# A sparse-attention and SwiGLU kernel: one identity copy moved from VectorE to ScalarE, and eight weight loads of 256 columns made into four of 512

## The chip, the cores and the metric

The kernel runs on one core of a Trainium2 chip. A core has a matrix engine (TensorE, PE in the profile), VectorE (DVE), ScalarE (ACT), GpSimd (POOL), and SyncE (SP), which here only issues DMAs. Each engine works through its own queue of instructions in order. Sixteen DMA engines move the data. The metric is the device time of one execution in microseconds.

## What is computed

Two stages follow each other. The first is block-sorted attention: for each of 4 batches and 8 heads an 8 x 8 matrix is normalised five times over rows and columns (Sinkhorn), its rows mix the eight 96-row blocks of k and v, and each block of q attends to its mixed block of k. The second is a SwiGLU feed-forward layer on the 3072 rows of 512 that come out.

```
P = sort_net
for _ in range(5):
    P = exp(P - max(P, -1));  P = P / sum(P, -1);  P = P / sum(P, -2)
k_sorted = einsum('bhij,bhjcd->bhicd', P, k_blocks)      # v the same
attn = softmax(q_blocks @ k_sorted.T / sqrt(64));  x = attn @ v_sorted
g = x @ w_gate;  val = x @ w_val                          # 512 -> 1536
out = (g * sigmoid(g) * val) @ w_out                      # 1536 -> 512
```

## The kernel before

All inputs lie in memory as 32-bit floats and are converted to bfloat16 by the DMAs that load them, which GpSimd issues (`load_v`, `load_k`, `load_q`, `load_gv`, and one load for `wo_sb`). The order of TensorE's and GpSimd's queues is the order of the program text, over the whole kernel; for VectorE and ScalarE that holds up to line 515, and later a scheduler orders them.

The start goes as follows. GpSimd issues the two halves of v of batch 0 (lines 134 and 135), builds the 128 x 128 identity `ident` (136), issues q and the four pieces of k of batch 0 (137 to 139), and then copies parts of v into `vch`, which holds v with its last two axes exchanged (140 to 142). A copy of one element of k's last piece into `landed` (144) makes it wait there until k is in. Then come the weight loads: `load_gv(lo, hi)` issues two DMAs, columns lo to hi of the gate weights into `wg_sb` and the same columns of the value weights into `wv_sb` (lines 145 to 149, with `load_v(1)` after column 1024). Behind them in the queue stand k and q of batch 1 and `wo_sb` (150 to 152), then the copies of v of batch 1 (573). The DMAs go around over eight completion semaphores, so an issue also waits for the load that used its semaphore eight loads earlier.

Meanwhile VectorE and ScalarE run the Sinkhorn loop (lines 183 to 200) on the tile `p_ps`: an exponential by ScalarE (184), then row sum, reciprocal, product, column sum, reciprocal, product by VectorE (194 to 200). In the second iteration VectorE also builds `mask` from `ident` (187) and copies a 64 x 64 corner of `ident` into the mixing matrix `rmix[0]` (188). That matrix is what TensorE multiplies k and q of batch 0 with (line 233): its upper half mixes k by P, its lower half passes q through. In the third and fourth iteration, and twice after the loop, ScalarE also takes its share of the copies into `vch` (`copy_v` with `nc.scalar`, lines 190, 192, 206 and 207). TensorE fills this time with matmuls on zeros (416, 420), some of them tied to the row sums (425).

Then v and k of batch 0 are mixed (`v_chunk`, `kq_chunk`), the scores, exponentials and products with v follow (`qk`, `av`), and the first half batch enters the feed-forward layer. The layer runs in eight passes n of 384 rows. A pass goes over twelve blocks m of 128 hidden columns: `gate(n, m)` (line 355 the matmuls, 363 tanh by ScalarE, 365 the product by VectorE) and `value(n, m)` (373 and 378). The blocks of pass 0 take their weights in column order: block m needs columns 128 m to 128 m + 127 of both matrices. Blocks 0 and 1 are started by `early` (497); the rest of pass 0 comes from `ffn(0)`, merged with attention work of the same batch by `merge`, which places side work by a running sum of costs. The product with `wo_sb` (390) of pass n comes in pass n + 1.

Of the kernel before, what the change touches and what calls it, by code (L numbers as in the profile page):

```python
# [17 lines left out]
def kernel(  # L18
# [11 lines left out]
    nc = tc.nc  # L30
# [9 lines left out]
    DF = moe_w_gate.shape[1]  # L40
# [50 lines left out]
    def load_k(b, lo, hi):  # L91
        rows = highr if b else lowr
        nc.gpsimd.dma_start(out=kq_tile(b)[rows, lo:hi, :], in_=k_nat[b, :, lo:hi, :])
# [10 lines left out]
    def load_v(b, lo, hi):  # L104
        if b // 2 not in v_tiles:
            v_tiles[b // 2] = vnp.tile([128, C, D], BF16, name=f"v{b // 2}", tag="vn")
        u = b % 2
        nc.gpsimd.dma_start(out=v_tiles[b // 2][u * R:(u + 1) * R, lo:hi], in_=v_nat[b, :, lo:hi, :])

    def load_w(sb, dram, lo, hi):  # L110
        nc.gpsimd.dma_start(out=sb[:, :, lo:hi], in_=dram[:, :, lo:hi])

    def load_gv(lo, hi):
        load_w(wg_sb, wg_dram, lo, hi)
        load_w(wv_sb, wv_dram, lo, hi)

    def copy_v(eng, pair, rows, s, n=4, d0=0, d1=D):
        cs = slice(s * (C // n), (s + 1) * (C // n))
        dst = vch3[rows, d0:d1, cs]
        src = v_tiles[pair][rows, cs, d0:d1]  # L120
        if eng is nc.scalar:
            eng.copy(dst, src.transpose([0, 2, 1]))
        else:
            eng.tensor_copy(dst, src.transpose([0, 2, 1]))  # L124

    ident = const.tile([128, 128], BF16)
    lowr, highr = slice(0, R), slice(R, 2 * R)
# [14 lines left out]
    copy_v(nc.gpsimd, 0, lowr, 5, 8, 40, D)  # L142
    landed = const.tile([R, 1], BF16)
    nc.gpsimd.tensor_copy(landed, kq_tiles[0][0:R, C - 1, D - 1:D])
    for m in range(0, 1024, 256):
        load_gv(m, m + 256)
    load_v(1, 0, C)
    for m in range(1024, DF, 256):
        load_gv(m, m + 256)
    load_k(1, 0, C)  # L150
    load_q(1, 0, C)
    nc.gpsimd.dma_start(out=wo_sb, in_=wo_dram)
# [1 line left out]
    rmix = {b: const.tile([128, 2, H, NB], BF16, name=f"rmix{b}") for b in (0, 1, "p")}  # L154
# [28 lines left out]
    for it in range(N_ITER):  # L183
        nc.scalar.activation(p_ps, p_sb if it == 0 else p_ps, AF.Exp)
        if it == 1:
            with nc.allow_low_precision("0/1 mask"):
                nc.vector.tensor_reduce(mask, id4, axis=AX.XY, op=ALU.add)
            nc.vector.tensor_copy(rmix[0][highr, 1].rearrange("p h i -> p (h i)"), ident[highr, highr])
        if it == 2:
            copy_v(nc.scalar, 0, lowr, 2, 8)  # L190
        if it == 3:
            copy_v(nc.scalar, 0, lowr, 3, 8)
        rowred = rowreds[it]
        nc.vector.reduce_sum(rowred[:, :, 0], p_ps, axis=AX.X)
        nc.vector.reciprocal(rowred, rowred)
        nc.vector.tensor_mul(p_ps, p_ps, rowred.to_broadcast([BH, NB, NB]))
        nc.vector.reduce_sum(colred[:, 0, :], p_ps.transpose([0, 2, 1]), axis=AX.X)
        nc.vector.reciprocal(colred, colred)
        if it < N_ITER - 1:
            nc.vector.tensor_mul(p_ps, p_ps, colred.to_broadcast([BH, NB, NB]))  # L200
# [428 lines left out]
```

## Time and profile before

Three runs gave 249.53, 249.59 and 250.57 us, a median of 249.59. The profiled execution has a span of 248.0 us; its own time beyond the span isn't recorded with the page, and the median lies 1.6 us above the span.

| what | us |
|---|---|
| median of the runs | 249.59 |
| span of the profiled execution | 248.0 |
| DVE busy | 157.7 |
| ACT busy | 110.3 |
| POOL busy | 52.5 |
| gate matmuls L355 | 76.5 |
| value matmuls L373 | 77.3 |
| output matmuls L390 | 64.0 |

Busy time is the time in which an engine executes; issuing a DMA doesn't count. The chain that ended last is followed back from the last instruction: at each step it goes to what released the instruction, or to the one before it on the same engine. In a timeline, the columns are the start in us, the length in us, the engine, the line of the kernel, the operation, the tile written and the tiles read, shapes and types, and how many instructions were merged; in brackets stands idle time of the engine before it and what ended it. A row for a DMA issue gives the issuing engine, the number of issues, the size and the time from the issue to the landing.

### The profile page before, as it was taken

How to read it: one execution, taken by the hardware profiler on the slowest of the kernel's cores; microseconds unless marked ns; L12 is line 12 of the kernel's file. 1: busy time of each engine (PE TensorE's matmuls, PEld its weight loads, DVE VectorE, ACT ScalarE, POOL GpSimd, SP SyncE). 2: the span in 40 equal slices, each digit the busy share in tenths (PEclk: the TensorE clock that was granted, in tenths of full speed). 3: DMA queues.
4: the chain of work that ended last, by engine and by line, in shares of the span. 5: the costliest groups of instructions: out<-in, count | busy, mean ns of one | idle time of the engine just before them, and what ended most of it. 6: DMA issues, size and time to landing. Idle time of an engine off the chain costs nothing.

```text
span 248.0 us, 6193 instructions
## 1 busy us (share of the span) xinstructions
PE 240.1 (97%) x2636; PEld 141.3 (57%) x2636; DVE 157.7 (64%) x332; ACT 110.3 (44%) x187; POOL 52.5 (21%) x47
## 2 busy tenths in 40 slices
PE   7899999999999999999999999999999999999994
PEld 6376566666555556655555655565555555555543
DVE  6778689887555775857657646755764585446700
ACT  2977553453544444454642552354244334232311
POOL 7948459960059200000000000000000000000000
PEclk9999999999999999999999999999999999999999
DMA  5959999999999296010122121112111121100122
GB/s 101 211 95 166 215 189 228 194 226 211 221 170 192 53 210 164 3 42 3 45 54 52 57 62 34 44 42 78 32 42 45 39 57 55 42 22 24 42 81 88
DMA packets 39530, 24.38 MB, mean 98 GB/s; under 512 B 27728, under 2 KB 35664, under 8 KB 38992
## 3 DMA queue, kind: packets, MB, share of 16 engines
q0 software_dynamic: 21328, 14.16, 38.9%
q1 hardware_dynamic: 18176, 9.84, 14.1%
q8 instruction: 20, 0.33, 0.5%
q14 instruction: 6, 0.05, 0.1%
HBM read 28.32 MB, written 7.86 MB: 146 GB/s over the span
## 4 chain that ended last, share of the span: by engine, by line
PE 83%; DVE 7%; ACT 3%; issue 3%; DMA 2%; DVEq 0%; ACTq 0%; POOLq 0%
PE v_ps L373 23%; PE o_ps L390 23%; PE g_ps L355 22%; PE tkq L233 4%; PE av_ps L304 3%; PE qk L277 2%; DVE gs_sb L365 2%; DMA v<-in_v_dram 2%; DVE st L310 2%; PE tv L245 2%; PE idle_ps L416 1%; DVE h L378 1%; PE o_ps L406 1%; ACT th_sb L363 1%; PE x_ps L321 1%
## 5 line engine op out<-in xcount | busy, mean ns | idle before, releaser
L365 DVE SCALAR_TENSOR_TENSOR gs_sb<-th_sb,g_ps 128x384 bf16<-128x384 bf16 x96 | 52.8, 550 | 51.8 <-ACT th_sb L363 49.1
L373 PE MATMUL v_ps<-xt,wv_sb 128*128 128x384 bf16 x380 | 77.3, 326 | 0.7 <-DVE gs_sb L365 0.4
L355 PE MATMUL g_ps<-xt,wg_sb 128*128 128x384 bf16 x376 | 76.5, 326 | 0.0
L363 ACT ACTIVATE th_sb<-g_ps 128x384 bf16<-128x384 f32 x96 | 47.1, 490 | 56.0 <-PE g_ps L355 53.5
L390 PE MATMUL o_ps<-wo_sb,h 128*128 128x512 bf16 x276 | 64.0, 379 | 0.0
L378 DVE SCALAR_TENSOR_TENSOR h<-v_ps,gs_sb 128x384 bf16<-128x384 f32 x96 | 53.3, 556 | 6.6
L373 PEld LDWEIGHTS <-wv_sb 128*128 128x128 bf16 x380 | 35.4, 97 | 24.6 <-issue 2.3
L355 PEld LDWEIGHTS <-wg_sb 128*128 128x128 bf16 x376 | 34.6, 97 | 23.2 <-issue 0.3
L390 PEld LDWEIGHTS <-h 128*128 128x128 bf16 x276 | 26.3, 98 | 28.9
L395 ACT COPY o_sb<-o_ps 128x512 f32<-128x512 f32 x23 | 13.5, 585 | 50.8 <-PE o_ps L390 50.8
L124 POOL COPY vch<-v 64x1536 bf16<-64x1536 bf16 (+2 forms) x11 | 28.6, 2639 | 20.7 <-DMA v<-in_v_dram 20.7
L290 ACT ACTIVATE e_all<-qk 96x768 bf16<-96x768 f32 x30 | 22.6, 802 | 8.1 <-PE qk L277 8.1
L310 DVE TENSOR_TENSOR st<-av_ps,r_sb 96x512 bf16<-96x512 f32 x32 | 21.7, 679 | 0.2
L304 PEld LDWEIGHTS <-e_all 96*128 96x128 bf16 x256 | 12.2, 98 | 4.9 <-ACT e_all L290 0.8
L304 PE MATMUL av_ps<-vt,e_all 96*128 96x65 bf16 x256 | 13.5, 194 | 0.0
L211 DVE CAST vt<-tv 96x1024 bf16<-96x1024 f32 (+1 forms) x9 | 9.8, 1100 | 2.7 <-PE tv L255 1.6
L308 DVE RECIPROCAL r_sb<-av_ps 96x8 f32<-96x8 f32 x32 | 6.4, 199 | 7.6 <-PE av_ps L304 7.5
L213 ACT CAST vt<-tv 96x1024 bf16<-96x1024 f32 (+1 forms) x9 | 9.2, 1032 | 3.1 <-PE tv L255 1.8
L211 DVE CAST kqt<-tkq 128x1024 bf16<-128x1024 f32 (+1 forms) x7 | 7.5, 1068 | 2.7 <-PE tkq L233 2.6
L213 ACT CAST kqt<-tkq 128x1024 bf16<-128x1024 f32 (+1 forms) x7 | 6.0, 894 | 6.6 <-PE tkq L233 6.6
L416 PE MATMUL idle_ps<-warm_sb 128*128 128x512 bf16 x28 | 8.7, 409 | 0.0
L233 PE MATMUL tkq<-rmix,kq 128*64 128x64 bf16 x384 | 7.8, 197 | 0.6 <-issue 0.6
(74 smaller groups left out, 126.3 us busy)
## 6 DMA issues: line engine op xcount, KB each, us to landing
out_dram<-o_sb SPq DMA_DIRECT2D x23, 256.0 KB, 2.0
v<-in_v_dram POOLq DMA_DIRECT2D x3, 768.0 KB, 19.9
kq<-in_q_dram POOLq DMA_DIRECT2D x2, 768.0 KB, 13.6
wg_sb<-in_moe_w_gate_dram POOLq DMA_DIRECT2D x6, 256.0 KB, 8.5
wv_sb<-in_moe_w_val_dram POOLq DMA_DIRECT2D x6, 256.0 KB, 9.1
wo_sb<-in_moe_w_out_dram POOLq DMA_DIRECT2D x1, 1536.0 KB, 23.8
kp<-in_k_dram POOLq DMA_DIRECT2D x2, 768.0 KB, 15.1
q_scr<-in_q_dram POOLq DMA_DIRECT2D x2, 768.0 KB, 29.9
```

Of the source, the lines that this page charges most:

```text
L124: eng.tensor_copy(dst, src.transpose([0, 2, 1]))
L211: nc.vector.tensor_copy(dst, src)
L233: nc.tensor.matmul(tp[two * D:(two + 1) * D, lc, :], lhsT=kq_tiles[b][:, at + lc, :], rhs=rm[:, two], start=True, stop=True)
L290: nc.scalar.activation(e_all[:, n:n + 2, 0:4 * C], wide[0:C, :, 0:4 * C], AF.Exp, scale=scale)
L304: nc.tensor.matmul(o[:, two, i4, :], lhsT=e[:, i4 * C:i4 * C + 128], rhs=vt[:, 2 * g + two, half * 4 + i4, :], start=True, stop=True)
L310: nc.vector.tensor_tensor(st.rearrange("p i two d -> p two i d"), o[0:C, :, :, 0:D], r_sb.to_broadcast([C, 2, 4, D]), op=ALU.mult)
L355: nc.tensor.matmul(g_ps, lhsT=wg_sb[:, kc, ts(m, 128)], rhs=xt[:, kc, :], start=(kc == 0), stop=(kc == NKC - 1))
L363: nc.scalar.activation(th_sb, g_ps, AF.Tanh, scale=0.5)
L365: nc.vector.scalar_tensor_tensor(gs_sb, th_sb, 1.0, g_ps, op0=ALU.add, op1=ALU.mult)
L373: nc.tensor.matmul(v_ps, lhsT=wv_sb[:, kc, ts(m, 128)], rhs=xt[:, kc, :], start=(kc == 0), stop=(kc == NKC - 1))
L378: nc.vector.scalar_tensor_tensor(h_tiles[n][:, m, :], v_ps, 0.5, gs_tiles.pop(m), op0=ALU.mult, op1=ALU.mult)
L390: nc.tensor.matmul(o_ps, lhsT=h_w[:, m, ts(t3, 128)], rhs=wo_sb[:, m, :], start=(m == 0), stop=(m == NFC - 1))
```

## The change

The copy of the identity corner goes from VectorE's queue to ScalarE's, between the second and the third exponential. The gate and value weights of columns 0 to 511 are loaded as before, those from column 512 on in loads of 512 columns: gate 512 to 1023, value 512 to 1023, v of batch 1, gate 1024 to 1535, value 1024 to 1535. That is eight weight loads rather than twelve, for the same bytes.

```
-    for m in range(0, 1024, 256):
-        load_gv(m, m + 256)
+    load_gv(0, 256)
+    load_gv(256, 512)
+    load_gv(512, 1024)
     load_v(1, 0, C)
-    for m in range(1024, DF, 256):
-        load_gv(m, m + 256)
+    load_gv(1024, DF)
...
-            nc.vector.tensor_copy(rmix[0][highr, 1].rearrange("p h i -> p (h i)"), ident[highr, highr])
+            nc.scalar.copy(rmix[0][highr, 1].rearrange("p h i -> p (h i)"), ident[highr, highr])
```

On the other engines the order of instructions stays what it was.

## The prediction

> **What bounds the kernel now.** I read the page first, for the engine shares and the DMA queues; then the chain of waits around the stage in which the first edit sits; then the timelines of VectorE, TensorE and GpSimd over the first 45 us, with the landing times of the weight loads.
>
> ```profile
> PE 240.1 (97%) x2636; PEld 141.3 (57%) x2636; DVE 157.7 (64%) x332; ACT 110.3 (44%) x187; POOL 52.5 (21%) x47
> PE   7899999999999999999999999999999999999994
> DMA  5959999999999296010122121112111121100122
> q0 software_dynamic: 21328, 14.16, 38.9%
> ```
>
> TensorE is busy for 97% of the span, from about 25 us on without a gap that matters. Its order is written out by hand, so a stall of TensorE in there moves all that follows. The DMA engines are full from slice 2 to slice 13 (6.2 us each). Whatever is asked for in that stretch lands in queue order, and asking sooner brings nothing.
>
> The first edit sits ahead of that, in the Sinkhorn loop, where TensorE runs filler. The chain of waits there:
>
> ```profile
> 1.27 4.98 DMA v<-in_v_dram
> 6.25 0.02 issue
> 6.28 1.53 ACT vch L122
> 7.81 0.12 ACT p_ps L184
> ```
>
> Up to 7.9 us the end is set by the landing of the first half of v (1.27 + 4.98 = 6.25), then by ScalarE's transposing copy of it, then by the fourth exponential, which stands behind that copy on ScalarE. VectorE's first two iterations are not in the chain. Its timeline:
>
> ```profile
> 3.84 0.22 DVE L200 TENSOR_TENSOR p_ps<-p_ps,colred 32x64 f32<-32x64 f32 x1
> 3.98 0.26 DVE L187 TENSOR_REDUCE mask<-ident 128x8 bf16<-128x128 bf16 x1
> 4.26 0.32 DVE L188 COPY rmix<-ident 64x64 bf16<-64x64 bf16 x1
> 4.61 0.21 DVE L194 TENSOR_REDUCE rowred<-p_ps 32x8 f32<-32x64 f32 x1
> ...
> 7.47 0.22 DVE L200 TENSOR_TENSOR p_ps<-p_ps,colred 32x64 f32<-32x64 f32 x1
> ```
>
> **The copy on ScalarE: what it removes.** In the second iteration the row sum L194 starts 0.77 us after L200 (4.61 - 3.84); the timeline has 0.48 us in the third iteration (6.28 - 5.80) and in the fourth (7.95 - 7.47). So the copy costs VectorE 0.29 us here, and without it L200 of the third iteration would start at 7.18 rather than 7.47 and the fourth exponential could follow at 7.44. But line 190's copy is ahead of that exponential in ScalarE's queue. It starts at 6.28 because v lands at 6.25, and its 1.53 us end at 7.81. The exponential started at 7.73 (successive ScalarE instructions overlap by 0.07 to 0.08 in the timeline: 7.73 + 0.19 against 7.85) and can't start sooner by more than 0.02. What is late next is therefore DMA, and the 0.29 us becomes waiting. I take a gain of 0.02. Its bounds are 0 and 0.29; the whole would need v to land by 5.96.
>
> **What it adds.** ScalarE gets one 64x64 copy. The trace has none from SBUF at this size there; the nearest rows are w_sb<-w_ps 64x64 at 0.21 us (L446) and 64x128 at 0.26 us (L447). I take 0.21. It would run from 4.31 to 4.52, while ScalarE sits idle for 1.78 us before the third exponential at 6.06 (5.77 then). Queued behind it is only that exponential, and 1.25 us of cover remain; without the cover it would cost 0.21. It needs ident, which GpSimd finishes at 3.04 (2.75 + 0.29). The sum for this edit is -0.02.
>
> **The weight loads: what is removed.** Eight loads of 256 columns, 256 KB each as written, become four of 512 KB. GpSimd spends 0.74 to 0.80 us on the issue of each. If a wide one costs the same (the row of wo, with three times the rows, took 1.05), four issues or some 3 us go; the bounds are 2 us and 3 us. None of it reaches the end: after its last issue GpSimd waits 2.62 us for v of batch 1 anyway. Behind these issues in its queue stand load_v(1), load_k(1), load_q(1) and wo. They are issued sooner into a full queue, and land when their bytes come.
>
> **What is moved: the landings.** A load reports as a whole. The value weights of column 1024, needed first, came in a load of their own and now wait for those of column 1535. Issues and landings, from GpSimd's timeline and the DMA view of each issue:
>
> ```profile
> 25.85 0.74 POOL L111 DMA_DIRECT2D wg_sb<-in_moe_w_gate_dram  x1 [0.59 <-DMA wv_sb<-in_moe_w_val_dram]
> 27.25 0.74 POOL L111 DMA_DIRECT2D wv_sb<-in_moe_w_val_dram  x1 [0.66 <-DMA wg_sb<-in_moe_w_gate_dram]
> ...
> wv_sb<-in_moe_w_val_dram POOLq DMA_DIRECT2D x1, 256.0 KB, 13.7
> wo_sb<-in_moe_w_out_dram POOLq DMA_DIRECT2D x1, 1536.0 KB, 23.8
> ```
>
> The last value load landed at 27.25 + 13.7 = 40.95. In the same way the four loads of columns 512 to 1023 landed at 26.95, 28.29, 29.62 and 31.05 (gate and value in turn), v at 34.78, and the last four at 35.99, 37.22, 38.55 and 40.95. Bytes keep their order except that gate's second half now goes before value's first. At the old rate the four new loads land where the second of each pair did: gate 512 at 28.29, value 512 at 31.05, gate 1024 at 37.22, value 1024 at 40.95. TensorE first needs them at 31.61, 32.61, 38.48 and 39.13, the starts of hidden blocks 4 and 8:
>
> ```profile
> 32.61 0.81 PE L373 MATMUL v_ps<-xt,wv_sb 128*128 128x384 bf16 x4
> ...
> 38.48 0.81 PE L355 MATMUL g_ps<-xt,wg_sb 128*128 128x384 bf16 x4
> 39.13 0.81 PE L373 MATMUL v_ps<-xt,wv_sb 128*128 128x384 bf16 x4
> ```
>
> Three keep a margin (3.3, 1.6 and 1.3 us). The fourth was 1.91 us early (39.13 - 37.22) and would be 1.82 us late. Two things change this.
>
> First, rows twice as long move faster. The wo load has the new row length. By bandwidth, the stretch from 35 to 38 us (narrow loads) moved 199 GB/s and that from 48 to 53 us (wo) 209: 2 MB take 10.5 or 10.0 us, 0.5 saved. By landings, wo came 7.02 us after q (31.29 + 23.8 = 55.09, against 29.87 + 18.2 = 48.07), 2.34 us for each 512 KB; four narrow loads at the pace of 35.99 to 38.55 (1.28) make 2.56. Over four wide loads that saves 0.9; at the slower pace of 25.52 to 31.05 (1.38, or 2.76 a pair) it would be 1.7. Bounds: 0 and 1.7. TensorE waits for landings, so I take 0.9: 40.05.
>
> Second, the last value load took 2.40 us after the one before it, against 1.28: 1.1 us of irregularity. Between 36 and 39 us the instruction queue has one 16 KB packet with 1.9% of 16 engines' 3 us, so 0.9 us of one engine. I take that fetch to follow the program, which is nearly the same after, so I leave the 1.1 us in; without it the load would land at 38.95, and nothing would be late.
>
> A weight load normally lies under the matmul before it; one that waits shows its 0.10 us (the page's 97 ns). The stall is 40.05 + 0.10 - 39.13 = 1.02 us, with bounds of 0 and 1.92 (40.95 + 0.10 - 39.13). Behind it stand the whole rest of TensorE's queue, and ScalarE, VectorE and the stores that feed on it. The chain of waits runs on TensorE alone from 30.96 to 61 us, so no gap gives the stall back. Sum: 1.02 - 0.02 = 1.0 us.
>
> **Rules against the rows.** Landings of narrow loads lie 1.28 us apart because they queue behind each other without a fixed price. [...]
>
> **The sum.** The page gives the span, 248.0; the median of the runs, 249.59, is 1.6 above it, which I take as constant around the span. Span 249.0, time 250.6.
>
> **The rivals.** (a) The stall of about 0.4 to 1.25 us, as summed: 250.6, chance 0.45. (b) Hidden anyway: wide rows and no irregularity, the load in time for block 8. For it speaks that only the last landing in the row of loads was uneven; against it that margin would be 0.1 to 0.2 us. Time 249.6, chance 0.21. (c) Slower by a measurable amount: the wide load brings no rate, the DMA engines being bound by what they read, and value 1024 lands at 40.95 or later, 1.8 us after TensorE wants it. For it speaks the step of only 199 to 209 GB/s. It decides from a landing after 40.28 (39.13 + 1.25 - 0.10). Time 251.4, chance 0.27. (d) The first edit does what it says: v lands earlier than in this profile, 0.29 us comes through, and the weights are in time: 249.3, chance 0.03. (e) Faster by something no row shows, 248.0: chance 0.04.
>
> **How the numbers follow.** A measurement of this kernel can tell some 0.5%, 1.25 us, from no change: below 248.34 faster, above 250.84 slower. Faster is (e), 0.04; slower is (c) and a little of (a), 0.28; the rest, 0.68, is the same. The range runs from 249.4, below (b) and near (d), to 251.6, just past the upper bound of the stall (249.59 + 1.92 = 251.5).
>
> **What would show it.** Right: the fourth exponential still at 7.7 us, with ScalarE waiting for DMA; a single TensorE gap of about 1 us ahead of block 8's value matmuls, released by the DMA of wv_sb, which lands near 40. Wrong: no gap there, or gaps at block 4 too, or a p_ps chain 0.29 us earlier at line 203. The time would be wrong if landings shift by more than a microsecond between executions.

## The result, and the profile after

The changed kernel took 251.92 us as the median of six runs (251.22 to 253.06), the kernel before 249.84 (six runs, 249.53 to 250.57). The ratio is 1.0081, with an interval of 1.0054 to 1.0107: slower by 2.1 us, and outside the range that was given. The profiled execution took 251.52 us with a span of 249.7, so 1.8 us lie outside the span. For the kernel before that was put at 1.6, as its median less the span of its profile; but executions of it with a span of 248.0 took 250.02 to 250.09 us in the batches of the experiments, so some 2.05 lie outside, and the profile came from an execution about 0.45 us slower than the median of 249.59. One of the twelve executions of e2 below (256.29 us, at a mean granted clock of 0.978) was in a slower state than the others and isn't counted.

From the page of the changed kernel, the shares of the engines, the DMA packets and the group of the value matmuls (busy us, mean ns of one, then idle time ahead and what ended it):

```profile
PE 237.6 (95%) x2611; PEld 141.2 (57%) x2636; DVE 157.6 (63%) x331; ACT 110.5 (44%) x188; POOL 49.5 (20%) x43
DMA packets 37418, 24.38 MB, mean 98 GB/s; under 512 B 27664, under 2 KB 33552, under 8 KB 36880
L373 PE MATMUL v_ps<-xt,wv_sb 128*128 128x384 bf16 x380 | 77.3, 326 | 3.2 <-DMA wv_sb<-in_moe_w_val_dram 2.5
```

GpSimd's 3 us are gone (52.5 to 49.5, x47 to x43: for GpSimd the page does count the issues of DMAs as busy time), as worked out, and so are 2112 DMA packets (39530 to 37418). The value matmuls now have 2.5 us of idle time that a weight load ended. Where it stands is seen in the chain of waits and in TensorE's timeline:

```profile
21.97 18.97 DMA wv_sb<-in_moe_w_val_dram
40.94 0.05 issue
40.99 0.82 PE v_ps L373 x4
```

```profile
24.23 0.48 PE L497 MATMUL g_ps<-xt,wg_sb 128*128 128x384 bf16 x2
...
37.71 0.81 PE L355 MATMUL g_ps<-xt,wg_sb 128*128 128x384 bf16 x4
40.99 0.82 PE L373 MATMUL v_ps<-xt,wv_sb 128*128 128x384 bf16 x4 [2.46 <-DMA wv_sb<-in_moe_w_val_dram]
```

The gap is where it was forecast: ahead of block 8's value matmuls, and nowhere else in the feed-forward layer's first pass. Two of its terms were not what was forecast. The load landed at 40.94, no sooner than the last narrow load of before. And TensorE came to the feed-forward layer at 24.23 instead of 25.00, so it was ready for block 8's values at 38.36 (37.71 + 0.65) instead of 39.13. It lost 40.99 - 38.36 = 2.63 us there, less the 0.77 that it had come sooner: 1.86, against 1.7 in the spans.

ScalarE's timeline in the Sinkhorn loop:

```profile
4.32 0.24 ACT L188 COPY rmix<-ident 64x64 bf16<-64x64 bf16 x1
5.79 0.19 ACT L184 ACTIVATE p_ps<-p_ps 32x64 f32<-32x64 f32 x1 [1.22 <-DVE p_ps L200]
6.20 1.52 ACT L122 COPY vch<-v 64x768 bf16<-64x768 bf16 x1 [0.23 <-DMA v<-in_v_dram]
7.63 0.20 ACT L184 ACTIVATE p_ps<-p_ps 32x64 f32<-32x64 f32 x1
```

The third exponential is 0.27 us sooner (5.79 against 6.06). Then ScalarE waits 0.23 us for v, and the fourth is 0.10 sooner (7.63 against 7.73), of which 0.08 is v's own landing (6.20 against 6.28). The moved copy took 0.24 us and nothing waited for it.

### The profile page after: what moved, and what is told of

It is laid out like the page before. It is cut to its first block, busy times and chain, and to the rows that moved or that the text cites. A ratio compares the mean times of both kernels' runs of the same rounds, so it can differ in the third digit from the quotient of the medians.

```text
span 249.7 us, 6164 instructions
## 1 busy us (share of the span) xinstructions
PE 237.6 (95%) x2611; PEld 141.2 (57%) x2636; DVE 157.6 (63%) x331; ACT 110.5 (44%) x188; POOL 49.5 (20%) x43
## 2 busy tenths in 40 slices
DMA packets 37418, 24.38 MB, mean 98 GB/s; under 512 B 27664, under 2 KB 33552, under 8 KB 36880
## 4 chain that ended last, share of the span: by engine, by line
PE 73%; DMA 12%; DVE 5%; POOL 4%; issue 3%; ACT 2%; DVEq 0%; POOLq 0%
PE o_ps L390 22%; PE v_ps L373 21%; PE g_ps L355 20%; DMA wv_sb<-in_moe_w_val_dram 8%; DMA kq<-in_k_dram 4%; PE tkq L233 3%; PE av_ps L304 2%; DVE gs_sb L365 2%; PE qk L277 2%; DVE h L378 1%; POOL wg_sb L111 1%; PE o_ps L406 1%; DVE st L310 1%; DVE vt L211 1%; POOL wv_sb L111 1%
## 5 line engine op out<-in xcount | busy, mean ns | idle before, releaser
L390 PE MATMUL o_ps<-wo_sb,h 128*128 128x512 bf16 x255 | 61.5, 379 | 1.3 <-issue 0.3
L233 PEld LDWEIGHTS <-kq 128*64 128x64 bf16 x384 | 6.8, 112 | 1.8 <-issue 1.5
```

The lines of the kernel that those rows point to most:

```text
L233: nc.tensor.matmul(tp[two * D:(two + 1) * D, lc, :], lhsT=kq_tiles[b][:, at + lc, :], rhs=rm[:, two], start=True, stop=True)
L390: nc.tensor.matmul(o_ps, lhsT=h_w[:, m, ts(t3, 128)], rhs=wo_sb[:, m, :], start=(m == 0), stop=(m == NFC - 1))
```

## The experiments

All ratios are to the kernel before, run on the same chip among the others, with 95% intervals. Four chips were used, one each for e1 to e4, e5 to e8, e9 and e10, and e11 and e12; the kernel before had medians of 249.71 to 250.07 on them, so medians of different batches compare to some 0.4 us only. The landing is that of the load with the value weights of column 1024; for the kernel before and the copy alone, the last value load's landing stands in brackets.

| run | ratio | median us | gap at block 8 in the profile, us | landing, us |
|---|---|---|---|---|
| before | 1 | 249.84 | 0 | 37.22 (40.95) |
| the change | 1.0081 (1.0054 to 1.0107) | 251.92 | 2.46 | 40.94 |
| e1 copy alone | 1.0004 (0.9978 to 1.0030) | 250.03 | 0 | 38.38 (42.26) |
| e2 wide loads alone | 1.0093 (1.0055 to 1.0131) | 251.43 | 1.19 | 40.03 |
| e3 middle pair wide | 0.9994 (0.9971 to 1.0017) | 249.53 | 0 | 36.99 |
| e4 last pair wide | 1.0137 (1.0081 to 1.0193) | 253.82 | 2.24 | 40.80 |
| e5 change, filler in the gap | 1.0074 (1.0045 to 1.0104) | 251.56 | 0.86 after the filler | 41.51 |
| e6 last values narrow again | 1.0019 (0.9993 to 1.0045) | 250.37 | 0.50 | 39.33 |
| e7 middle wide, v in halves | 0.9989 (0.9968 to 1.0011) | 249.58 | 0 | 35.91 |
| e8 change, v in halves | 1.0000 (0.9975 to 1.0025) | 249.57 | 0.20 | 38.59 |
| e9 a third of wo first | 1.0054 (1.0034 to 1.0075) | 251.36 | 1.73 | 40.60 |
| e10 narrow, v in halves | 0.9995 (0.9976 to 1.0013) | 249.65 | 0 | 35.64 |
| e11 e4 with filler | 1.0083 (1.0049 to 1.0118) | 251.83 | 0.15 after the filler | 40.96 |
| e12 e4 again, beside e11 | 1.0129 (1.0076 to 1.0181) | 253.71 | 2.38 | 41.27 |

### Which edit, and which load

The first four separate the parts. e1 has only `nc.scalar.copy` in line 188, e2 only the wide loads. e3 and e4 have the copy and one wide pair each:

```
e3:  load_gv(512, 1024); load_v(1, 0, C); load_gv(1024, 1280); load_gv(1280, DF)
e4:  load_gv(512, 768); load_gv(768, 1024); load_v(1, 0, C); load_gv(1024, DF)
```

> Copy on ScalarE alone, all weight loads 256 columns wide. Theory A (the copy takes a hole out of the k mixing): the 0.57 us gap of TensorE near 17 us in the profile of before is gone, the first gate matmul (line 497) starts near 24.2 instead of 25.0, and the time falls by 0.6 to 0.8 us, ratio 0.997. Theory B (the hole is chance of the one profile): the Sinkhorn chain gives at most 0.1 us, ratio 0.9995 to 1.000, and the hole is there in some profiles and not in others.

> Wide loads alone, the copy on VectorE as before. Both theories: one TensorE gap ahead of block 8's value matmuls, released by the load of wv_sb, which lands near 40.9. Theory A: TensorE arrives at 39.1, the gap is 1.8 to 1.9 us and the time rises by that, ratio 1.0075. Theory B: arrival is between 38.4 and 39.1 by chance, and the end is set by the landing alone, so this kernel takes as long as the whole change, ratio 1.008.

> Copy on ScalarE, columns 512 to 1023 in wide loads, columns from 1024 on in loads of 256. If the last pair of wide loads alone makes the stall, there is no gap at block 8 and the time is that of the copy alone, ratio 0.997 to 1.000; the value load of 512 to 1023 lands near 31.2, ahead of block 4 (32.6 or 31.8). If the middle pair has a part in it, a gap shows at block 4, or block 8's loads land later than 36 and 37.2.

> Copy on ScalarE, columns 512 to 1023 in loads of 256, columns from 1024 on in wide loads. If the last pair makes the whole stall: a gap of 1.8 to 2.5 us ahead of block 8's value matmuls and the time of the whole change, ratio 1.007 to 1.008. If wide rows of the middle pair had saved any landing time, the last load would land up to 0.5 later here than in the whole change (40.9).

The copy alone changes nothing that can be measured. The gap near 17 us is still in its profile, at 0.34 us, so theory A falls. Wide loads alone are as slow as the whole change by the ratio; their median of 251.43 says less, because the eleven executions fall into two groups (250.60 to 251.43 and 253.27 to 254.25), which the next section takes up. The middle pair costs nothing in e3, as its margins of 3.3 and 1.6 us said, and the last pair makes the loss. TensorE's timeline in e2, e3 and e4, in this order:

```profile
40.08 0.82 PE L373 MATMUL v_ps<-xt,wv_sb 128*128 128x384 bf16 x4 [1.19 <-DMA wv_sb<-in_moe_w_val_dram]
```

```profile
38.33 0.81 PE L374 MATMUL v_ps<-xt,wv_sb 128*128 128x384 bf16 x4
```

```profile
40.84 1.20 PE L374 MATMUL v_ps<-xt,wv_sb 128*128 128x384 bf16 x4 [2.24 <-DMA wv_sb<-in_moe_w_val_dram]
```

In e3 the block starts at 38.33 and waits for nothing. In e4 two things stand out: a median 1.9 us above that of the change, and four matmuls that take 1.20 us instead of 0.82.

### The clock after the wait

Those longer matmuls led to e5 and, later, to the pair e11 and e12. The filler is one line among the side work of pass 0, ahead of `value(0, 8)`; it computes nothing that is used:

```
+            if n == 0 and m == 8:
+                todo.append((0.0, lambda: fill(bank_tile("gap_ps", "x"), 9)))
```

> The whole change, with nine filler matmuls of 128x512 (0.22 us each, 1.9 us in all) in TensorE's queue between block 8's gate and value matmuls, where the wait for the load lies. If the wait alone sets the end (1.2 to 2.5 us by the landing), the filler lies inside it and the time is 251.2 to 251.5, as in the undisturbed runs of the change. If a part of the change's time comes from the granted clock falling after the wait (half clock for 3.4 us in the profile of the wide last pair alone, worth 1.7 us), that part goes: no execution with a mean clock of 0.993, none above 252, and the median is 251.3 against 251.9 for the change and 252.3 for wide loads alone. If the clock has nothing to do with it, the spread up to 254 stays.

> The wide last pair alone (as in e4) with nine filler matmuls (2.1 us) in TensorE's queue between block 8's gate and value matmuls. If the clock falls because TensorE is idle there, few executions or none have a mean granted clock of 0.993, and the median is 251.2 to 251.6, about what the executions of e4 at full clock took (251.5 and 251.7). If the fall has another cause, about half or more stay at 0.993 and the median near e12's.

> The same kernel as e4, beside e11 on the same chip: half or more of the executions at a mean clock of 0.993 and 253 to 255 us, the others at 1.000 and 251 to 252; median 252.5 to 254.

The view by stages of e12 (busy us and count of each engine, then PEclk, the granted clock, DMA share and GB/s):

```profile
39.00:41.00 2.00, 0.00 (x0) 0.00 (x0) 0.80 (x2) 0.47 (x1) 2.00 (x2) 1.00 1.11 221
41.00:42.00 1.00, 0.68 (x4) 0.46 (x5) 0.00 (x0) 0.00 (x0) 1.00 (x2) 0.90 1.00 209
42.00:43.00 1.00, 1.00 (x12) 0.69 (x10) 0.17 (x2) 0.00 (x0) 1.00 (x1) 0.50 1.00 209
43.00:44.00 1.00, 1.00 (x5) 0.50 (x4) 1.00 (x3) 0.00 (x0) 1.00 (x1) 0.50 1.10 233
44.00:45.00 1.00, 1.00 (x5) 0.47 (x4) 0.42 (x2) 0.49 (x1) 1.00 (x2) 0.50 1.04 221
45.00:46.00 1.00, 1.00 (x10) 0.60 (x8) 0.63 (x3) 0.00 (x0) 1.00 (x1) 0.89 0.76 154
```

TensorE is idle from 39 to 41 us and works again at 41.32, after a wait of 2.38 us for the weights; from 41.80 to 45.22 the clock is at half. The lost shares, 0.10 + 0.50 + 0.50 + 0.50 + 0.11, make 1.71 us of full-speed work. The same sum in e4 is 0.43 + 0.50 + 0.50 + 0.28 = 1.71. In e11 the filler takes the wait's place, and the matmuls behind it run at full speed:

```profile
38.74 2.10 PE L417 MATMUL gap_ps<-warm_sb 128*128 128x512 bf16 x9
41.00 0.82 PE L374 MATMUL v_ps<-xt,wv_sb 128*128 128x384 bf16 x4 [0.15 <-DMA wv_sb<-in_moe_w_val_dram]
```

The mean granted clock is listed for every execution. Without filler it was 0.991 to 0.993 in 2 of 6 of the change, 5 of 11 of e2, 4 of 6 of e4, 4 of 6 of e12 and none of 6 of e9 (the whole change with a part of wo moved, below), and 0.998 or more in the rest. With filler it fell in 1 of 9 (e5) and 0 of 8 (e11). Beside each other on one chip, e11 has a median of 251.83 and e12 253.71: 1.9 us, near the 1.71 of the stages. With one edit between them, 0 of 8 against 4 of 6, idle TensorE is thus shown as the cause of the clock's fall at block 8. e5 alone wouldn't show it: its median of 251.56 was expected at 251.3, its interval overlaps that of the change, and three of its nine executions took over 252 us at a clock of 0.999 or more (one of e11's took 254.44 at 0.999). So the clock doesn't explain every long time. One execution of e10, whose profile waits for no weights, fell to 0.993 too; why is open.

Within the change itself, the two executions at 0.993 took 252.78 and 253.06, the other four 251.22 to 252.32. In e2 and e4 the two groups lie some 3.1 us apart (medians 250.87 and 253.95, 251.61 and 254.67), more than 1.71. What makes the rest isn't shown, since no kernel has a trace of each kind.

A wait of 2.46 us left the clock alone (the profile of the change), and one of 2.24 didn't (e4). The traces show the difference. They record when the granted clock changes. In e4 the record of the full clock starts at 7.01 us, and the fall comes at 41.15, ten times 3.413 us later; in e12 the two are 4.26 and 41.80, eleven times 3.413 apart, and both falls last 3.41. The profile of before records the full clock from 6.64 us on for 242.35 us, 71 times 3.413, and that of the change from 5.60 on for 245.76, 72 times; half clock follows in both, behind the last instruction. So TensorE's work can be summed in steps of that length, here for e4, e12 and the change, two steps each (the step, its length, busy us and count of TensorE, then as above):

```profile
37.73:41.15 3.42, 1.18 (x7) 1.00 1.22 242
41.15:44.56 3.41, 3.41 (x20) 0.50 0.97 205
```

```profile
38.39:41.80 3.41, 1.03 (x7) 1.00 1.15 229
41.80:45.22 3.42, 3.42 (x20) 0.50 1.02 216
```

```profile
36.32:39.73 3.41, 2.20 (x20) 1.00 1.30 237
39.73:43.15 3.42, 2.16 (x20) 1.00 1.03 216
```

In e4 and e12 the wait lies within one step, which is left with 1.18 and 1.03 us of matmuls, and the next step runs at half clock. In the change the wait lies across two steps, which are left with 2.20 and 2.16 us, and no fall follows. The last steps of the program agree: 0.57 us of work in e8's (243.68 to 247.10) and 0.94 in e1's (244.08 to 247.49) are followed by half clock, 1.70 in e9's (244.56 to 247.97) isn't. So in these rows half clock comes after steps with 0.57 to 1.18 us of work and not after those with 1.70 to 2.20. That the work within a step decides is an estimate from these few steps; no run moves the steps alone. They lie differently in each of these three executions (the full clock's record starts at 4.26 us in e12, 5.60 in the change and 7.01 in e4), and with them, by this estimate, whether a wait of this length costs 1.7 us more.

### Which part of the order

e6 leaves the gate weights wide and takes the value weights from column 1024 on in two loads. e8 is the whole change with v of batch 1 in two halves, the second behind the last weights; e7 has the same halves with narrow last pairs, and e10 with narrow loads throughout.

```
e6:  load_w(wg_sb, wg_dram, 1024, DF); load_w(wv_sb, wv_dram, 1024, 1280); load_w(wv_sb, wv_dram, 1280, DF)
e8:  load_gv(512, 1024); load_v(1, 0, HC); load_gv(1024, DF); load_v(1, HC, C)
```

> The whole change, but the value weights from column 1024 on again in two loads of 256; gate weights stay wide. If what matters is only that value 1024 waits for value 1535, the load for block 8 lands 1.2 to 1.5 sooner (38.6 to 39.5 against 40 to 40.9), the gap shrinks to 0.2 to 1.1 us, no clock fall follows, and the time is 250.0 to 250.8, ratio 1.001 to 1.004. If the order (gate's second half ahead of value's first) makes most of it, the gap stays above 1.5 and the time above 251.

> The whole change, with load_v(1) cut in two, the second half behind the wide last pair. The landing of the last value load comes 1.9 us sooner, 38.1 to 39.0 against 40.0 to 40.9, while TensorE arrives at 38.4 to 39.1. If the landing alone makes the change slower, the gap falls to 0 to 0.6 us, the clock stays full and the time is 249.4 to 250.2, ratio 0.998 to 1.002. If the wide loads cost something else besides, the time stays above 250.8.

TensorE's timeline at block 8 in e6 and in e8:

```profile
39.38 0.82 PE L375 MATMUL v_ps<-xt,wv_sb 128*128 128x384 bf16 x4 [0.50 <-DMA wv_sb<-in_moe_w_val_dram]
```

```profile
38.64 0.82 PE L374 MATMUL v_ps<-xt,wv_sb 128*128 128x384 bf16 x4 [0.20 <-DMA wv_sb<-in_moe_w_val_dram]
```

e6 brings the landing to 39.33 and the time to within 0.5% of before, with the gate weights still in front of the values. So most of the loss is that the first half of the values waits for the second. That the order makes a smaller part rests on the gap of 0.50 us in one profile; the interval of e6 includes no loss at all. e8 has both wide pairs and the time of before, 1.0000: within 0.25% the wide loads cost nothing but the late landing. Its second half of v is still in time for GpSimd's copies, which start on it at 40.45.

> Copy on ScalarE, columns 512 to 1023 wide, from 1024 on narrow, and load_v(1) cut in two, the second half behind the last weights. All weights of blocks 8 to 11 land 1.9 us sooner (half of v's 3.8), so no execution has a gap at block 8 or 10. If the spread of before (249.2 to 251.7) comes from such late landings, it shrinks to 249.1 to 249.8 and the median falls to 249.4, ratio 0.998. If v is then late for GpSimd's copies, a gap shows ahead of the v mixing (line 245, near 47.7) and the time rises.

> Copy on ScalarE, all weight loads 256 wide, load_v(1) cut in two with the second half behind the last weights: the version with the most margin at blocks 4, 8 and 10. If late weights are what spreads the times of before, no execution waits for weights, the median is 249.3 and the spread 248.9 to 249.9, ratio 0.996 to 0.998. If the spread comes from elsewhere, it stays at 249.0 to 251.5 and the ratio at 0.998 to 1.001.

Neither beats the kernel before by more than its interval. In e10 no matmul of the feed-forward layer waited for weights in the profile, and its runs spread from 249.17 to 251.31 all the same. So the expectation that late weights spread the times of before finds no support; what spreads them is open. In e7 a gap of 0.41 us stood at block 4 instead, where the wide middle value load landed at 32.28: a margin of 1.6 us in one profile was used up in another.

### Why the last load lands so late

e9 puts a third of the wo load between the last value load and k of batch 1:

```
+    nc.gpsimd.dma_start(out=wo_sb[:, 0:4], in_=wo_dram[:, 0:4])
     load_k(1, 0, C)
     load_q(1, 0, C)
-    nc.gpsimd.dma_start(out=wo_sb, in_=wo_dram)
+    nc.gpsimd.dma_start(out=wo_sb[:, 4:], in_=wo_dram[:, 4:])
```

> The whole change, with a third of the wo load (four of its twelve row blocks, 512 KB in rows like those of the wide loads) put between the last value load and k of batch 1. Theory C (the last load's slow end comes from what stands behind it: engines that are through go over to k's long packets and take the bandwidth of those still at weights): the spread of the sixteen engines' ends of that load falls from 1.3 to 3.0 us to 1.6 or less, it lands at 40.0 or before, and the time falls to 250.3 to 251.0. Theory D (the slow end is made by something that hits single engines, such as the 16 KB instruction fetch near 37 us): spread and landing stay at 1.3 to 3.0 and 40.0 to 41.5, and the time at 251.2 to 252.4. k and q of batch 1 then land 2.5 us later (46.7 and 50.6), ahead of their use near 54.

```profile
40.65 0.66 PE L374 MATMUL v_ps<-xt,wv_sb 128*128 128x384 bf16 x3 [1.73 <-DMA wv_sb<-in_moe_w_val_dram]
```

The landing came at 40.60 and the sixteen engines' ends were 2.0 us apart in the one profile, within theory D's numbers and outside theory C's. The median, 251.36, is in D's range too, at its low end. The long packets of k are thus not needed for a late landing. That a packet of the instruction queue makes it isn't shown by this: two explanations were set against each other and one fell.

## Why the prediction was wrong

**The first edit: right.** -0.02 us was forecast, with a bound of -0.29; the copy alone has a ratio of 1.0004, whose interval (-0.55 to +0.75 us) can't tell the two apart. The timelines can: VectorE's saving came through up to the third exponential and ended in ScalarE's wait for v, as the chain of waits said.

**Issues and GpSimd: right.** In the profile of the change a wide load took 0.79 to 0.83 us to issue, in that of before a narrow one 0.74 to 0.80. The issue set nothing: e4 issued its last value load at 23.94, 1.97 us later than the change, and it landed at 40.80, no later than the change's 40.94.

**Place and mechanism of the stall: right.** Block 8's values, one load that reports as a whole, no gap at block 4, nothing given back later: the profile of the change, e3, e4, e6 and e8 agree with these. Only e7 had a gap at block 4.

**The landing: its step failed.** "TensorE waits for landings, so I take 0.9: 40.05." The seven executions profiled with the wide last pair in its place gave 40.94, 40.03, 40.80, 41.51, 40.60, 40.96 and 41.27, a mean of 40.9. Six are later than forecast. The pace of wo, one load with its neighbours' unevenness in its landing, was taken for the price of a long row. The bandwidth row gave 0.5 and was the better one. The same stretch, with narrow loads before and with wide ones in the change (the last number is GB/s):

```profile
35.00:38.00 3.00, 3.00 (x42) 1.00 1.45 199
35.00:38.00 3.00, 3.00 (x29) 1.00 1.24 208
```

So the rate rose as forecast by bandwidth, which would put the landing at 40.45. What is left is the spread: the last value load's sixteen engines ended 1.3 to 3.0 us apart in the seven profiles, and TensorE waits for the slowest (in the change, fifteen had ended by 40.31 and the last at 40.94; block 8's values started at 40.99). The prediction had named this sign itself: "The time would be wrong if landings shift by more than a microsecond between executions." (That the DMA engines are full from slice 2 to 13 was misread too: slice 3, 12.4 to 18.6 us, has a 5. Nothing in the sum rests on it.) Nor is the old landing of 40.95 a fixed number: narrow loads landed last at 40.98 in e3 and 42.26 in e1, where block 10 waited for 0.38 us:

```profile
42.31 0.82 PE L373 MATMUL v_ps<-xt,wv_sb 128*128 128x384 bf16 x4 [0.38 <-DMA wv_sb<-in_moe_w_val_dram]
```

**The need: mis-sized.** 39.13 was read off the one profile, whose TensorE had lost 0.57 us near 17 us to a gap that the thirteen other profiles have shorter or not at all. In the profile of the change the need was at 38.36, in e2 and e11 near 38.7. Where the landing sets the end, an earlier TensorE only waits longer. So the forecast difference to before was too small by as much as that profile's execution was slower than the median to which the stall was added, some 0.45 us. The two sizes together turn 1.02 into 1.2 to 2.5 us.

**The granted clock: not in the sum at all.** The step "so no gap gives the stall back" asked whether a stall could shrink, not whether it could grow. At half clock for 3.4 us it grew by 1.71 in the profiles of e4 and e12, and the mean clock is at 0.991 to 0.993 in 15 of the 35 executions with the wide last pair behind the whole of v and no filler. This is what carries the median from about 251.4 (the change's undisturbed level, 251.22 to 251.52 in three of four) to 251.92, and past the upper end of the range, 251.6, which had counted 1.92 us of stall and no clock: with 1.71 us taken off the two executions at 0.993, the six would have a median of 251.4, an estimate. So the landing and the need explain why the time lies above 250.6, and the clock why it lies outside the range.

**The rivals.** (c), 251.4 by an unchanged landing, was the nearest in time, and its chance of 0.27 too small; but its reason, that wide loads bring no rate, is not what happened (199 to 208 GB/s). (b), hidden anyway, appears only in e8, when v makes room. A fixed price for each load finds no support: e3, with two loads fewer, has 0.9994, and e8, with four weight loads fewer, 1.0000.

## What to carry to other kernels

Before loads are merged, write down for each the landing of its last byte and the start of the first instruction that needs its first byte; a margin smaller than the landing's spread between executions (here 1.5 us over seven profiles) is no margin. Take both times from several profiles, and price a stall of an otherwise busy TensorE with the half-clock stretch that may follow (here 1.71 us in e4 and e12, where the 3.41 us ahead of it held 1.18 and 1.03 us of matmuls). What a removed instruction saves on a chain is what is left of it at the next wait for something that didn't move: here a DMA.

## What the runs showed of the hardware

TensorE's gap near 17 us always stands after the same matmul, the ninth of a chunk. In the fourteen profiles, seven have the gap (0.16 to 0.57 us) and seven don't. The second 16 KB packet of the instruction queue started at 14.77 to 15.20 us in the seven with it (15.20 in that of before), and at 14.38 to 14.60 in the seven without (14.38 in that of the change). That is a correlation without an exception, not an experiment: no kernel here moved that packet alone, and what makes the gap isn't shown.

Late ends of a weight load stood beside such packets in two profiles. The sixteen engines report their ends one by one in the trace. In the profile of the change, fifteen had finished the first gate load by 20.14 us and the last one at 21.43, which is when the load landed; a packet of the instruction queue had started at 18.70 and taken 1.33 us. In e2 it was 20.42 and 21.49, with a packet at 19.25 of 1.08 us. In e8 and e10 a packet started at 19.37 and 19.38, beside the end of the first gate load (19.74 and 19.82), and its sixteen ends were only 0.5 us apart. The trace doesn't tell on which engine a packet ran, so no link between the two is shown. Whether the late ends near 40 us (40.14 to 40.94 for the last four in the change) come from the packet near 37 (36.64 there) stays open as well.
